# Sign bits of two heads in one matmul run, from two-head tiles loaded for them, with the instruction order drawn anew

## The chip, the cores and the metric

The kernel runs on one core of one Trainium2 chip. The metric is device time in microseconds (us) of one execution, lower is better, as the median of three runs. The engines are named as in the profile: PE is the matrix engine (TensorE), PEld its weight loads, DVE the vector engine, ACT the scalar engine, POOL the GpSimd engine, SP the engine that issues most DMAs.

## The reference

Attention of 2 x 8 heads with 768 tokens of 64 numbers, in which a query sees only the keys of its hash bucket. Then two feed-forward layers on the 1536 x 512 result, the first with a leaky ReLU, the second with a rational function of its input.

```python
def _attn_ref(q, k, v, proj):            # 2 x 8 x 768 x 64, proj 64 x 6
    q_bits = (np.einsum('bhsd,dk->bhsk', q, proj) > 0).astype(np.int64)
    k_bits = (np.einsum('bhsd,dk->bhsk', k, proj) > 0).astype(np.int64)
    powers = 2 ** np.arange(n_bits)      # 6 bits
    mask = np.sum(q_bits * powers, -1)[:, :, :, None] == np.sum(k_bits * powers, -1)[:, :, None, :]
    scores = np.where(mask, scale * np.matmul(q, k.transpose(0, 1, 3, 2)), -1000000000.0)
    attn = np.exp(scores - np.max(scores, axis=-1, keepdims=True))
    attn = attn / (np.sum(attn, axis=-1, keepdims=True) + 1e-09)
    return np.matmul(attn, v)
# layer 1: h = x @ w_in (512 -> 2048); g = max(h,0) + alpha*min(h,0); g @ w_out
# layer 2: h = x @ w_in; P = cubic(h); Q = 1 + |b0||h| + |b1|h*h; (P / (Q + 1e-6)) @ w_out
```

## The kernel before, in words

**Attention.** The 16 heads go one after the other. `head(h)` loads the head's transposed keys and queries, `rk` and `rq` (128 x 768: the head's 64 rows, twice one below the other), makes a rounded copy of each (`k2`, printed as `k`, and `qh`) and the remainders (`kx`, `ql`). The bucket test rides in the score matmul: rows 64 to 75 of `ql` and `k2` hold the 6 sign bits and their complements of each query and key, scaled so that each bit that differs adds a huge penalty.

**Bits.** `bits_mm` (L452) projects the head on the 6 vectors and their negatives in four small matmuls into one PSUM tile `pb`, two column halves of q and two of k; the trace counts each matmul twice. `bits_ev` (L457) turns `pb` into bits `bt` in one DVE instruction, and `move` (L468) copies `bt` by four small DMAs from SP to rows 64 to 75 of `ql` and `k2`; for head 0 DVE writes them there itself (L461). The weights `zq` and `zk` have rows for the upper 64 partitions only, the rest is zero.

**Rows of a head.** For each of 6 tiles of 128 queries: scores `s` on PE (L520, L522), clamp and row maximum `x` on DVE (L528), exponential on ACT (L534), transposition `t` on PE (L552), copy to `pt` (ACT mostly). Then P times V into `pv` (L612, two pieces of 12 trace rows or one of 24), and the row sums: their reciprocals are split in two parts `rr`, turned by PE into `rb` (L584), copied to `rt`, spread by PE (L591), copied to `rs`, and multiplied in (L619, `acc`).

**Layers.** Each weight arrives as 64-bit pieces `raw` that ACT and DVE turn into two 32-bit parts (L304 to L334); in attention about one piece per head is done between the heads' work. Layer 1 and 2 run in units of 512 tokens and a quarter of the hidden width: matmuls `h` (L641), the nonlinearity on ACT, DVE and POOL (L677 to L721), its two parts `gh` and `gl`, matmuls `o` (L657 in layer 1, L660 in layer 2), and a sum on DVE (L764). Four PSUM buffers `h` hold the hidden values until `gl` (L419) has been made.

**Order.** Nothing of the order is written by hand. `plan.add` hands over tasks with the buffers that they read and write and a duration for each engine that may do them; `Plan.order` is a list scheduler that gives every task an engine and a place. The table `FAVOUR` shifts each kind of task: a number added to its rank, and a factor on its duration by engine. Another table gives another order, and other engines for the copies. A DMA is queued on SP in the planned order, and SP waits at each for its buffer. `CAP` sets the number of buffers, and `SP` here is also the name of a DRAM scratch (`sp`).

Of the kernel before, what the change touches and what calls it, by code (L numbers as in the profile page):

```python
# [14 lines left out]
ALU = mybir.AluOpType  # L15
# [17 lines left out]
PAD = 16  # L33
# [9 lines left out]
CAP = {"raw_qk": 2, "qh": 2, "kx": 2, "ql": 2, "k2": 2, "bt": 2, "vr": 2,  # L43
# [26 lines left out]
    "backb": (12.5, {"act": 0.05, "dvp": 0.48}), "banks": (-9.8, {"none": 1.11}), "bits": (6.4, {"pe": 2.45}),  # L70
    "bits0": (307.2, {"pe": 1.69}), "bits_at": (284.5, {"dvp": 0.31}), "bits_ev": (25.3, {"dvp": 0.3}),
    "bits_evb": (30.6, {"dvp": 2.87}), "bits_mv": (-7.6, {"dma": 2.11}), "bits_mvb": (47.1, {"dma": 0.57}),
    "bitsb": (451.7, {"pe": 0.94}), "c_abs": (293.3, {"act": 0.63}), "c_bits": (-40.2, {"dve": 5.95}),
    "c_hi": (-2525.5, {"act": 0.33, "dve": 0.06, "pool": 0.4}), "c_lo": (-27.6, {"dve": 0.24}),
    "c_load": (191, {"dma": 0.12, "none": 3.41}), "c_prep": (673.4, {"dve": 0.7}), "c_tail": (1.1, {"act": 0.38}),
    "clamp": (24.3, {"dvp": 2.08}), "clampb": (-181.2, {"dvp": 8.19}), "e_abs": (65.7, {"act": 2.31}),
    "e_bits": (-1115.9, {"dve": 0.36}), "e_lo": (15.6, {"dve": 1.15}), "e_load": (124.3, {"dma": 0.27}),
    "e_out": (415.1, {}), "e_tail": (-137.8, {"act": 0.42}), "expo": (30, {"act": 0.67}), "expob": (0, {"act": 1.51}),
    "eye": (-1276, {"dma": 2.17}), "eye_prep": (333.9, {"act": 0.02, "dve": 0.04, "pool": 0.04}),
# [5 lines left out]
    "g_lo0": (0, {"dvp": 0.28}), "g_lo1": (-1009.1, {"dvp": 1.07}), "g_lo2": (130.7, {"dvp": 0.85}),
    "g_neg": (-317, {"act": 1.54}), "g_neg0": (-112.5, {"act": 6.17}), "g_neg1": (-1.8, {"act": 7.94}),
    "guard": (86.4, {}), "guardb": (-505.3, {"dve": 1.6}), "k2": (0, {"act": 3.0, "dve": 0.42, "pool": 0.18}),
    "k20": (97, {"act": 0.02, "dve": 50.0, "pool": 0.19}), "k2b": (145.6, {"act": 0.74, "dve": 5.4, "pool": 1.68}),
    "kx": (0.7, {"dve": 2.0}), "kx0": (-2.6, {}), "kxb": (-355, {"dve": 8.17}), "load": (-1817.5, {"dma": 8.2}),
    "load0": (0, {"dma": 0.78, "none": 0.34}), "loadb": (66.1, {"dma": 2.11}), "o_add1": (-656.2, {"dvp": 2.93}),  # L90
    "o_add2": (-19.4, {}), "o_ev": (-181.6, {"act": 1.85, "dvp": 1.35}), "o_ev0": (150.6, {"act": 0.07, "dvp": 50.0}),
    "o_ev2": (330.1, {"act": 0.22, "dvp": 1.37}), "over": (-33.2, {"dvp": 0.04}), "overb": (-457.4, {"dvp": 0.48}),
    "part1": (-74.5, {"act": 4.65, "dve": 0.09, "pool": 0.81}),
    "part1b": (13.8, {"act": 4.7, "dve": 0.03, "pool": 2.52}), "part2": (52.2, {"dve": 9.8, "pool": 4.83}),
# [160 lines left out]
def lsh_attention_moe_moe(ctx: ExitStack, tc: tile.TileContext, qT, kT, vN, consts, eye,  # L255
# [119 lines left out]
    cp.tile([128, PAD], F32, name="pad")  # L375
# [11 lines left out]
    Z = [hp.tile([128, 32], F32, name=f"z{n}") for n in "qk"]  # L387
# [35 lines left out]

    def head(h):
# [33 lines left out]

        def bits_at(n):
            to, j, r = T["ql" if n < 2 else "k2"], n % 2, slice(32 * n, 32 * n + 2 * NB)  # L460
            v_.tensor_scalar(to[64:64 + 2 * NB, j * HALF:(j + 1) * HALF], T["b"][r, :HALF],  # L461
                             cst[r, 0:1], cst[r, 1:2], op0=ALU.is_ge, op1=ALU.mult)

        def move(n):
            def f(e):
                for j in range(2):
                    r = 64 * n + 32 * j
                    nc.sync.dma_start(out=T[("ql", "k2")[n]][64:64 + 2 * NB, j * HALF:(j + 1) * HALF].bitcast(F32),  # L468
                                      in_=T["bt"][r:r + 2 * NB].bitcast(F32))
            return f  # L470
# [531 lines left out]
```

## Time and profile before

| | |
|---|---|
| median of 3 runs | 775.31 us (774.53 to 777.95) |
| the profiled execution | 774.81 us, of which its span 773.0 us |
| PE busy | 760.3 us, 98% of the span |
| DVE, ACT, POOL busy | 650.1 (84%), 542.5 (70%), 147.7 (19%) |
| granted PE clock | 0.998 of full speed |
| attention | until about 256 us; layer 1 until about 495 us, layer 2 after it |

The time is 1.81 us more than the span, which runs from the first to the last instruction. An engine's busy time counts overlapping instructions once.

### The profile page before, as it was taken

How to read it: one execution, taken by the hardware profiler on the slowest of the kernel's cores; microseconds unless marked ns; L12 is line 12 of the kernel's file. 1: busy time of each engine (PE TensorE's matmuls, PEld its weight loads, DVE VectorE, ACT ScalarE, POOL GpSimd, SP SyncE). 2: the span in 40 equal slices, each digit the busy share in tenths (PEclk: the TensorE clock that was granted, in tenths of full speed). 3: DMA queues.
4: the chain of work that ended last, by engine and by line, in shares of the span. 5: the costliest groups of instructions: out<-in, count | busy, mean ns of one | idle time of the engine just before them, and what ended most of it. 6: DMA issues, size and time to landing. Idle time of an engine off the chain costs nothing.

```text
span 773.0 us, 11054 instructions
## 1 busy us (share of the span) xinstructions
PE 760.3 (98%) x3868; PEld 600.4 (78%) x3868; DVE 650.1 (84%) x1208; ACT 542.5 (70%) x945; POOL 147.7 (19%) x135
## 2 busy tenths in 40 slices
PE   8999999999999999999999999989999999999998
PEld 6776777677677788888888888868888888888886
DVE  6899988988887797998899989998787787787882
ACT  4998898798787465643454455788998887777770
POOL 2231211231300000000000000044333343323330
PEclk9999999999999999999999999999999999999999
DMA  6333434545411223345632563520201400200012
GB/s 211 110 108 124 142 94 146 167 128 168 149 60 42 69 81 109 110 138 162 190 101 91 171 208 97 207 98 39 109 1 52 166 1 1 109 1 2 14 55 95
DMA packets 27127, 79.69 MB, mean 103 GB/s; under 512 B 3696, under 2 KB 4416, under 8 KB 25536
## 3 DMA queue, kind: packets, MB, share of 16 engines
q1 hardware_dynamic: 26784, 78.58, 31.2%
q8 instruction: 30, 0.49, 0.2%
q10 hardware_dynamic: 288, 0.41, 0.2%
q14 instruction: 25, 0.20, 0.1%
HBM read 62.14 MB, written 15.73 MB: 101 GB/s over the span
## 4 chain that ended last, share of the span: by engine, by line
PE 90%; DVE 6%; ACT 2%; issue 1%; DMA 0%; POOL 0%; SPq 0%; DVEq 0%; POOLq 0%
PE h L641 33%; PE o L660 17%; PE o L657 14%; PE pv L612 7%; PE t L552 7%; PE s L520 4%; PE s L522 4%; PE pb L452 2%; PE h L657 1%; DVE x L528 1%; PE warm L790 1%; DVE kx L444 1%; PE rb L591 1%; DVE h L703 1%; DVE acc L619 0%
## 5 line engine op out<-in xcount | busy, mean ns | idle before, releaser
L641 PE MATMUL h<-xh,wih 128*128 128x512 f32 x384 | 150.6, 392 | 2.9 <-DVE gl L419 2.9
L641 PE MATMUL h<-xh,wil 128*128 128x512 f32 x384 | 150.1, 391 | 0.0
L641 PE MATMUL h<-xl,wih 128*128 128x512 f32 x384 | 150.0, 391 | 0.0
L706 POOL TENSOR_TENSOR x<-x,ap 128x512 f32<-128x512 f32 x48 | 62.1, 1295 | 284.9 <-DVE ap L706 283.1
L528 DVE TENSOR_SCALAR_CACHE_REDUCE x<-s 128x768 f32<-128x768 f32 x96 | 91.2, 952 | 7.7 <-PE s L522 6.1
L534 ACT ACTIVATE x<-x,st 128x768 f32<-128x768 f32 x96 | 89.4, 933 | 7.7 <-DVE x L528 7.1
L410 ACT ACTIVATE gh<-h 128x512 fp32r<-128x512 f32 x95 | 56.6, 597 | 47.7 <-DVE h L721 27.8
L641 PEld LDWEIGHTS h<-xh,wih 128*128 128x128 f32 x384 | 72.4, 188 | 18.3 <-DVE gl L419 3.3
L641 PEld LDWEIGHTS h<-xl,wih 128*128 128x128 f32 x384 | 72.5, 189 | 15.2
L641 PEld LDWEIGHTS h<-xh,wil 128*128 128x128 f32 x384 | 72.5, 189 | 15.0
L410 ACT ACTIVATE pt<-t 128x768 f32<-128x768 f32 x96 | 76.6, 804 | 10.6 <-PE t L552 9.8
L552 PE MATMUL t<-eyes,x 128*128 128x128 f32 x576 | 79.9, 276 | 1.2 <-DVE x L528 0.7
L552 PEld LDWEIGHTS t<-eyes,x 128*128 128x128 f32 x576 | 64.5, 141 | 19.3 <-ACT x L534 9.9
L660 PE MATMUL o<-woh,gh 128*128 128x512 f32 x192 | 74.7, 389 | 0.0
L660 PE MATMUL o<-woh,gl 128*128 128x512 f32 x192 | 74.7, 389 | 0.0
L660 PE MATMUL o<-wol,gh 128*128 128x512 f32 x192 | 74.7, 389 | 0.0
L419 DVE TENSOR_TENSOR gl<-h,gh 128x512 fp32r<-128x512 f32 x96 | 64.6, 684 | 11.0 <-ACT gh L410 9.9
L657 PE MATMUL o<-gh,woh 128*128 128x512 f32 x176 | 68.5, 389 | 0.0
L657 PE MATMUL o<-gh,wol 128*128 128x512 f32 x176 | 68.5, 389 | 0.0
L657 PE MATMUL o<-gl,woh 128*128 128x512 f32 x176 | 68.5, 389 | 0.0
L612 PE MATMUL pv<-pt,vr 128*64 128x384 f32 x384 | 68.3, 494 | 0.0
L764 DVE TENSOR_TENSOR acc<-acc,o 128x512 f32<-128x512 f32 x72 | 48.9, 681 | 16.9 <-PE o L660 14.7
(114 smaller groups left out, 1488.7 us busy)
## 6 DMA issues: line engine op xcount, KB each, us to landing
raw<-w_in SPq DMA_DIRECT2D x32, 512.0 KB
raw<-w_out SPq DMA_DIRECT2D x32, 512.0 KB
rk<-kT SPq DMA_DIRECT2D x16, 384.0 KB
sp<-mag SPq DMA_DIRECT2D x24, 256.0 KB
rq<-qT SPq DMA_DIRECT2D x15, 384.0 KB
sp<-w SPq DMA_DIRECT2D x16, 256.0 KB
vr<-vN SPq DMA_DIRECT2D x8, 384.0 KB
wih<-sp SPq DMA_DIRECT2D x3, 1024.0 KB
```

The lines of the kernel that those rows point to most:

```text
L410: s_.activation(out, in_, AF.Copy, scale=scale)
L419: eng[e].tensor_tensor(out, a, b, op=ALU.subtract)
L520: te.matmul(sp[:, j, :HALF], K["qh"][:, q], K["kx"][:, j * HALF:(j + 1) * HALF], start=True, stop=False)
L528: v_.tensor_scalar(x.rearrange("p (j c) -> p j c", j=2), T["s"][:, :, :HALF], SCALE, FAR, op0=ALU.mult, op1=ALU.min, accum_out=T["st"])
L534: s_.activation(T["x"], T["x"], AF.Exp, bias=T["st"], scale=-1.0, accum_out=tr["ss"][:, tt, half:half + 1])
L552: te.transpose(o[:, c], T["x"][:, c], idf)
L612: te.matmul(T["pv"][64 * half:64 * half + 64, :HALF], tv["vr"][:, m, kt, :], E[half][0]["pt"][:, kt, :], start=(kt == 0), stop=(kt == NT - 1))
L641: te.matmul(hp, wt[:, kc, f], xt[:, kc], start=(n == 0), stop=(n == 3 * KC - 1))
L657: te.matmul(op, lt[:, m, d], rt, start=(n == 0), stop=(n == 3 * FT - 1))
L660: te.matmul(op, lt[:, d], rt[:, m], start=(n == 0), stop=(n == 3 * FT - 1))
L706: eng[e].tensor_tensor(P[a], P[a], P[b], op=op)
L764: v_.tensor_tensor(a, a, o, op=ALU.subtract if moe else ALU.add)
```

## The change

From head 2 on the bits of two heads (2 and 3, 4 and 5, ...) come from one run. For it the two heads' 64 rows stand one below the other in tiles of their own (`rp`), which two more loads per pair bring from new inputs `kN` and `qN`. The weights get a second block of 12 columns for the lower 64 rows, so `bits_mm` and `bits_ev` stay as they are, 4 matmuls and one evacuation, but yield 24 rows per group instead of 12. The heads' own tiles `rq`, `rk` are still loaded. `bt` has one buffer instead of two and serves both heads' moves; heads 0 and 1 keep their own runs. The `FAVOUR` table is new throughout. The planner's price of a move goes from 1.0 to 1.45.

```diff
-CAP = {"raw_qk": 2, "qh": 2, "kx": 2, "ql": 2, "k2": 2, "bt": 2, "vr": 2,
+CAP = {"raw_qk": 2, "qh": 2, "kx": 2, "ql": 2, "k2": 2, "rp": 2, "bt": 1, "vr": 2,
...
-    "scaled": (312, {"act": 0.17, "dvp": 21.96}), "scaledb": (-242.3, {"act": 2.09, "dvp": 0.42}),
...
+    "s22": (57.1, {}), "scaled": (-33, {"act": 12.9, "dvp": 0.39}), "scaledb": (118.7, {"act": 29.24, "dvp": 0.02}),
...
+        def load2(n, src):
+            def f(e):
+                P[n] = tl(hp, "rp", [128, S], F32, f"{n}{h}")
+                nc.sync.dma_start(out=P[n], in_=src[h // 2])
+            return f
...
-                r = T["rq" if n < 2 else "rk"]
-                te.matmul(T["b"][32 * n:32 * n + 32, :HALF], Z[n // 2], r[:, n % 2 * HALF:(n % 2 + 1) * HALF],
+                r = P["rq" if n < 2 else "rk"]
+                te.matmul(P["b"][32 * n:32 * n + 32, :HALF], Z[n // 2], r[:, n % 2 * HALF:(n % 2 + 1) * HALF],
...
-                    r = 64 * n + 32 * j
+                    r = 64 * n + 32 * j + h % 2 * 2 * NB * (h > 1)
...
-        b = plan.buf("b")
-        plan.add("bits" + z, bits_mm, {"pe": 0.98}, [*R, BZ], [b], cols=1536)
+        if h < 2:
+            P = T
+        elif h % 2 == 0:
+            P = PAIR[h // 2] = {}
+            R = [plan.buf("rp") for n in "kq"]
+            for n, src, r in (("rk", kN, R[0]), ("rq", qN, R[1])):
+                plan.add("load2" + z, load2(n, src), {"dma": 1.1}, writes=[r])
+        else:
+            P = PAIR[h // 2]
+        if h < 2 or h % 2 == 0:
+            b = plan.buf("b")
+            plan.add("bits" + z, bits_mm, {"pe": 0.98}, [*R, BZ], [b], cols=1536)
         if h:
-            bt = plan.buf("bt")
-            plan.add("bits_ev" + z, bits_ev, {"dvp": 0.6}, [b], [bt])
+            if h == 1 or h % 2 == 0:
+                P["B"] = plan.buf("bt")
+                plan.add("bits_ev" + z, bits_ev, {"dvp": 0.6}, [b], [P["B"]])
+            bt = P["B"]
             for n in range(2):
-                plan.add("bits_mv" + z, move(n), {"dma": 1.0}, [bt, *([B["kx"]] * n)], [B[("ql", "k2")[n]]])
+                plan.add("bits_mv" + z, move(n), {"dma": 1.45}, [bt, *([B["kx"]] * n)], [B[("ql", "k2")[n]]])
...
         for z, sign in zip(Z, (1.0, -1.0)):
-            for i in range(2):
-                v_.tensor_scalar(z[0:64, i * NB:(i + 1) * NB], every[0:64, 0:NB], sign * (1 - 2 * i), None, op0=ALU.mult)
+            for m in range(2):
+                for i in range(2):
+                    r, c = slice(64 * m, 64 * m + 64), (2 * m + i) * NB
+                    v_.tensor_scalar(z[r, c:c + NB], every[r, 0:NB], sign * (1 - 2 * i), None, op0=ALU.mult)
...
+        "qN": lay(inputs["q"].reshape(NH, S, D).transpose(0, 2, 1)).reshape(NH // 2, 2 * D, S),
+        "kN": lay(inputs["k"].reshape(NH, S, D).transpose(0, 2, 1)).reshape(NH // 2, 2 * D, S),
```

Line numbers of the changed kernel are 4 higher at `head`'s loads and 22 higher from the rows of a head on.

**PE, in the rows of head 2.** `s_2` and `s_3` are score tiles, `t_0` a transposition, `pb` the bits. Before, the run for head 3 stands here:

```order
L520 MATMUL s_2_545<-kx_323,qh_373 128x384 x2
L522 MATMUL s_2_545<-k_318,ql_109 128x384 x2
L552 MATMUL t_0_556<-eyes,x_0_519 128x128 x6
L452 MATMUL pb_568<-rq_481,zq 32x384 x2
L452 MATMUL pb_568<-rk_448,zk 32x384 x2
L520 MATMUL s_3_576<-kx_323,qh_373 128x384 x2
L522 MATMUL s_3_576<-k_318,ql_109 128x384 x2
```

Now:

```order
L542 MATMUL s_2_562<-kx_326,qh_379 128x384 x2
L544 MATMUL s_2_562<-k_323,ql_108 128x384 x2
L574 MATMUL t_0_571<-eyes,x_0_534 128x128 x6
L542 MATMUL s_3_582<-kx_326,qh_379 128x384 x2
L544 MATMUL s_3_582<-k_323,ql_108 128x384 x2
```

The two `pb` rows are gone. In the whole program `pb` has 36 matmuls instead of 64 (9 runs instead of 16), and `pv` stands in 30 pieces instead of 29.

**SP, the first loads.** Before, with `rk_193`, `rq_208` the tiles of head 1 and `eyes` the identity for the transpositions:

```order
L440 DMA rk_155<-kT 128x768
L502 DMA vr_157<-vN 128x768
L298 DMA raw<-w_in 128x512
L801 DMA eyes<-eye 128x512
L502 DMA vr_175<-vN 128x768
L298 DMA raw<-w_in 128x512
L440 DMA rk_193<-kT 128x768
L440 DMA rq_208<-qT 128x768
```

Now, with `rk_194`, `rq_207` the tiles of head 1 and `rk_175`, `rq_199` those of the pair 2 and 3:

```order
L444 DMA rk_154<-kT 128x768
L301 DMA raw<-w_in 128x512
L524 DMA vr_168<-vN 128x768
L454 DMA rk_175<-kN 128x768
L301 DMA raw<-w_in 128x512
L524 DMA vr_192<-vN 128x768
L444 DMA rk_194<-kT 128x768
L454 DMA rq_199<-qN 128x768
L825 DMA eyes<-eye 128x512
L444 DMA rq_207<-qT 128x768
```

The pair's two tiles stand ahead of head 1's queries, and `eyes` has moved behind head 1's keys.

**DVE, from layer 1 to layer 2.** Before, the last rows up to the second `gl` of layer 2 (`h<-t,bab,h`, `h<-h,qc,aq` and `h<-h,aq` are steps of layer 2's function, `mag`, `raw`, `wol` of a weight piece):

```order
L325 SCALAR_TENSOR_TENSOR mag<-raw 128x512
L703 SCALAR_TENSOR_TENSOR h<-h,aq 128x512
L319 TENSOR_SCALAR mag<-mag 128x512
L327 TENSOR_SCALAR raw<-c 128x512
L321 TENSOR_SCALAR mag<-mag 128x512
L697 SCALAR_TENSOR_TENSOR h<-t,bab,h 128x512
L721 TENSOR_TENSOR h<-x,h 128x512 x2
L764 TENSOR_TENSOR acc_62<-acc_62,o 128x512 x2
L334 SCALAR_TENSOR_TENSOR wol_100<-mag,raw 128x512
L419 TENSOR_TENSOR gl<-h,gh 128x512 x2
```

Now:

```order
L421 TENSOR_TENSOR gl<-h,gh 128x512
L326 SCALAR_TENSOR_TENSOR c<-raw,mag 128x512
L725 SCALAR_TENSOR_TENSOR h<-h,qc,aq 128x512
L322 TENSOR_SCALAR mag<-mag 128x512
L725 SCALAR_TENSOR_TENSOR h<-h,aq 128x512
L324 TENSOR_SCALAR mag<-mag 128x512
L743 TENSOR_TENSOR h<-x,h 128x512
L725 SCALAR_TENSOR_TENSOR h<-h,qc,aq 128x512
L719 SCALAR_TENSOR_TENSOR h<-t,bab,h 128x512
L421 TENSOR_TENSOR gl<-h,gh 128x512
```

From layer 2's first product `ap<-ap,t` to its second `gl` DVE has 34 instructions before and 29 now; PE's matmul groups stand in the same order here. Over the whole program the new table also gives DVE 16 copies `rs<-rb` instead of 5, 8 `ql<-qh,rq` instead of 1, 1 `rr<-ss` instead of 11 and none instead of 7 `rr<-ss,rr`, 5 `rt<-rb` instead of 9, no `qh<-rq` instead of 2, 8 `bt` instead of 15, 8 instructions for `zq` and `zk` instead of 4, and in layer 2 28 `x<-x,ap` instead of none and 33 `ap<-ap,t` instead of 24; those left to POOL are 20 instead of 48 and 15 instead of 24.

## Rows read from the trace of the kernel before

**Rows 1.** Stretches: us; busy PE, PEld, DVE, ACT, POOL (instructions); clock, DMA share, GB/s.

```profile
9.00:30.00 21.00, 17.59 (x102) 13.78 (x102) 19.81 (x41) 15.58 (x30) 6.34 (x6) 1.00 0.36 119
30.00:210.00 180.00, 178.35 (x1214) 124.55 (x1213) 163.16 (x359) 155.73 (x283) 40.74 (x41) 1.00 0.44 134
50.00:90.00 40.00, 39.81 (x272) 27.54 (x271) 38.53 (x86) 35.50 (x67) 9.46 (x12) 1.00 0.40 127
256.00:487.00 231.00, 231.00 (x1021) 191.25 (x1020) 207.33 (x378) 116.18 (x200) 1.24 (x2) 1.00 0.41 130
520.00:740.00 220.00, 220.00 (x964) 182.03 (x965) 171.65 (x266) 181.09 (x309) 80.65 (x63) 0.99 0.12 47
```

**Rows 2.** What PE waited for: us in total, times, longest; the largest.

```profile
PE h L641 <- DVE gl L419: 2.9, 1, 2.9
```

**Rows 3.** The chain that ended last, around two bits runs: start, length, what.

```profile
58.51 0.35 PE s L522 x2
58.86 0.78 PE pb L452 x8
59.64 0.80 PE t L552 x6
...
85.56 0.66 PE t L552 x6
86.21 0.78 PE pb L452 x8
87.00 0.55 PE s L520 x2
```

**Rows 4.** Groups by line and shape: count, busy us and mean ns, idle before.

```profile
L457 DVE TENSOR_SCALAR bt<-pb,every 128x384 fp32r<-128x384 f32 x15 | 10.1, 673 | 1.5 <-PE pb L452 1.5
L414 DVE COPY rs<-rb 128x384 f32<-128x384 f32 x5 | 2.7, 545 | 0.0
L419 DVE TENSOR_TENSOR ql<-qh,rq 64x768 fp32r<-64x768 f32 x1 | 1.0, 951 | 1.2 <-ACT qh L410 1.2
L414 DVE CAST rr<-ss 128x6 fp32r<-128x6 f32 x11 | 3.2, 293 | 0.6
L419 DVE TENSOR_TENSOR rr<-ss,rr 128x6 fp32r<-128x6 f32 x7 | 1.1, 160 | 0.1
L414 DVE CAST rt<-rb 12x128 fp32r<-12x128 f32 x9 | 2.5, 275 | 1.6 <-PE rb L584 1.6
L414 DVE CAST qh<-rq 128x768 fp32r<-128x768 f32 x2 | 1.1, 556 | 0.0
L706 DVE TENSOR_TENSOR ap<-ap,t 128x512 f32<-128x512 f32 x24 | 16.6, 692 | 16.7 <-ACT ap L694 16.5
```

**Rows 5.** The time line ahead of the wait in rows 2: start, length, instruction.

```profile
512.41 1.44 POOL L706 TENSOR_TENSOR ap<-ap,t 128x512 f32<-128x512 f32 x1 [2.00 <-ACT ap L694]
...
512.28 0.42 DVE L319 TENSOR_SCALAR mag<-mag 128x512 f32<-128x512 f32 x1
512.62 1.51 DVE L327 TENSOR_SCALAR raw<-c 128x512 uint32<-128x512 uint32 x1
514.05 1.51 DVE L321 TENSOR_SCALAR mag<-mag 128x512 uint32<-128x512 uint32 x1
```

**Rows 6.** The time line of the first tiles: landings that ended waits, ACT's first exponential.

```profile
10.54 0.65 ACT L308 ACTIVATE raw<-raw 128x512 uint32<-128x512 uint32 x1 [0.97 <-DMA raw<-w_in]
...
12.06 1.06 POOL L412 TENSOR_SCALAR k<-rk 128x768 fp32r<-128x768 f32 x1 [9.23 <-DMA rk<-kT]
...
15.15 0.94 ACT L534 ACTIVATE x<-x,st 128x768 f32<-128x768 f32 x1 [3.96 <-DVE x L528]
```

**Rows 7.** The time line of SP's moves for one head, and its first scores.

```profile
99.75 0.33 SPq L440 DMA_DIRECT2D rk<-kT  x1
...
102.74 1.47 SPq L468 DMA_DIRECT2D k<-bt  x2
...
106.35 0.59 PE L520 MATMUL s<-kx,qh 128*128 128x384 f32 x2
```

More of the change, by code (lines that the diff above doesn't have):

```diff
@@ L70 @@
[L70 to L79, printed above, removed]
@@ L85 @@
[L85 to L94, printed above, removed]
@@ new lines @@
+    "a_n2": (95.9, {"dvp": 0.84}), "a_p0": (-107.9, {"act": 3.65}), "a_p1": (-1736.7, {"act": 4.27}),
+    "a_prep": (-194.9, {}), "a_quad": (255.2, {"dvp": 0.98}), "a_sq": (-261.1, {"act": 2.63}),
+    "a_sum": (2279.3, {"dve": 0.07, "pool": 0.09}), "back": (274.2, {"act": 0.11, "dvp": 0.1}),
+    "backb": (58, {"act": 0.06, "dvp": 12.89}), "banks": (0, {"none": 1.11}), "bits": (346.6, {"pe": 2.45}),
+    "bits0": (211.4, {"pe": 1.69}), "bits_at": (-91.8, {"dvp": 0.31}), "bits_ev": (-316.4, {"dvp": 0.3}),
@@ new lines @@
+    "bits_evb": (0, {"dvp": 2.87}), "bits_mv": (12.7, {"dma": 2.11}), "bits_mvb": (-273.9, {"dma": 0.57}),
+    "bitsb": (91.1, {"pe": 0.94}), "c_abs": (-4.9, {"act": 0.63}), "c_bits": (95.1, {"dve": 5.95}),
+    "c_hi": (-503.4, {"act": 0.14, "dve": 0.03, "pool": 0.75}), "c_lo": (224.1, {"dve": 0.24}),
+    "c_load": (0, {"dma": 0.12, "none": 3.41}), "c_prep": (-9.9, {"dve": 0.7}), "c_tail": (-3.2, {"act": 0.38}),
+    "clamp": (-114.9, {"dvp": 2.08}), "clampb": (31.5, {"dvp": 8.19}), "e_abs": (505.1, {"act": 2.31}),
@@ new lines @@
+    "k20": (-173.3, {"act": 27.15, "dve": 6.82, "pool": 0.81}),
+    "k2b": (499.9, {"act": 0.02, "dve": 3.04, "pool": 0.03}), "kx": (-11.8, {"dve": 2.0}), "kx0": (-47.6, {}),
+    "kxb": (630.3, {"dve": 8.17}), "load": (12.6, {"dma": 8.2}), "load0": (63.4, {"dma": 0.78, "none": 0.34}),
+    "load2": (-185.6, {}), "load2b": (739.3, {}), "loadb": (-9.7, {"dma": 2.11}), "o_add1": (-1156.9, {"dvp": 2.93}),
+    "o_add2": (-17.3, {}), "o_ev": (205.6, {"act": 0.02, "dvp": 0.35}),
+    "o_ev0": (-518.2, {"act": 0.02, "dvp": 14.13}), "o_ev2": (125.4, {"act": 0.02, "dvp": 16.79}),
@@ new lines @@
+    "over": (-27.7, {"dvp": 0.04}), "overb": (-6.3, {"dvp": 0.48}),
+    "part1": (372.8, {"act": 0.03, "dve": 1.44, "pool": 3.09}),
+    "part1b": (-119.9, {"act": 0.04, "dve": 0.04, "pool": 16.03}), "part2": (-19.1, {"dve": 20.21, "pool": 0.14}),
+    "part2b": (-223.5, {"dve": 40.41, "pool": 0.02}), "pv": (-1426.8, {"pe": 1.11}), "pvb": (-1793.9, {}),
+    "qh": (-1018.2, {"act": 0.7, "dve": 2.98, "pool": 1.89}),
+    "qh0": (-12.9, {"act": 1.28, "dve": 6.94, "pool": 1.38}), "qhb": (-108, {"act": 2.22, "dve": 0.19, "pool": 0.06}),
@@ new lines @@
+    "scores": (-756.2, {"pe": 2.11}), "scoresb": (-431.8, {}), "spread": (7.8, {"pe": 2.26}),
+    "spreadb": (213.4, {"pe": 0.46}), "store": (-47.7, {}), "swap": (205.5, {}),
+    "take": (57, {"act": 0.17, "dvp": 4.39}), "takeb": (0, {"act": 3.25, "dvp": 26.81}),
+    "turn": (748.7, {"pe": 0.19}), "turnb": (-179.2, {"pe": 3.96}), "u_abs": (1021.6, {"act": 3.87}),
+    "u_bits": (-6.1, {}), "u_hi": (-15.7, {"act": 0.07, "dve": 6.47, "pool": 0.82}), "u_lo": (1.7, {"dve": 0.17}),
+    "u_load": (-346.3, {"dma": 0.33}), "u_tail": (297.4, {"act": 1.39}), "v_load": (-31.4, {"dma": 0.51}),
@@ L254, in lsh_attention_moe_moe @@
 @with_exitstack
-def lsh_attention_moe_moe(ctx: ExitStack, tc: tile.TileContext, qT, kT, vN, consts, eye,
+def lsh_attention_moe_moe(ctx: ExitStack, tc: tile.TileContext, qT, kT, qN, kN, vN, consts, eye,
                           w_in1, w_out1, w_in2, w_out2, out):
@@ L374, in lsh_attention_moe_moe @@
     rt = cp.tile([128, 128], F32R, name="rt")
-    cp.tile([128, PAD], F32, name="pad")
+    Z = [cp.tile([128, 32], F32, name=f"z{n}") for n in "qk"]
     att = ExitStack()
@@ L921, in swap_rest @@
         more(o=ps2, h2=ps2, mag2=mp, w322=cp, ap=mp, aq=mp)
-    for f, b, tags in ((swap, BS[1], ("raw_qk", "qh", "kx", "ql", "k2", "bt")),
+    for f, b, tags in ((swap, BS[1], ("raw_qk", "qh", "kx", "ql", "k2", "rp", "bt")),
                        (swap_rest, BS[2], ("x", "pt", "vr", "st", "ss", "rr", "rt", "rs", "s", "b", "pv", "h"))):
@@ L970 @@
     for n in range(4):
-        cst[32 * n + n // 2 * NB:32 * n + (n // 2 + 1) * NB, 0] = TINY
+        for m in range(2):
+            c = 32 * n + (2 * m + n // 2) * NB
+            cst[c:c + NB, 0] = TINY
         cst[32 * n:32 * n + 32, 1] = PEN if n > 1 else 1.0
```

69 lines of the change are left out of this document (32 added, 37 removed).

## The prediction

> **What bounds the kernel now.** I read the stretches first [rows 1]. PE is busy all the time from 256 to 487 us and from 520 to 740 us, and 178.35 of 180 us in attention proper (30 to 210 us). DVE comes next, with 163.16 of these 180 us, 90.6%. So a microsecond of PE work that goes from attention comes off the end, as long as DVE doesn't take over; where PE stands idle, a better order can give something back. The idle times lie at the start (3.4 us between 9 and 30 us), in attention (1.65 us), between the layers and at the very end. Of PE's named waits only one is long [rows 2]: 2.9 us for `gl` on DVE, once, where layer 2 begins. The sum is made against the profiled execution, 774.81 us (a span of 773.0 us and 1.81 us around it).
>
> **The removed bits runs.** Seven of 16 runs go, those of heads 3, 5, ... 15. In the chain a run takes 0.78 us from its start to the next group [rows 3]. The group behind it pays too: six transpositions take 0.80 us there and 0.66 us elsewhere, two score matmuls 0.55 us and 0.35 us elsewhere. That is 0.14 to 0.20 us more, so 0.95 us a run, 6.65 us for seven. One more piece of `pv` costs one such extra, 0.20 us. Left: **-6.45 us**, if PE's work sets the end there; nothing, if DVE does. These runs are matmul work that nothing covers, so no cover is lost with them.
>
> **DVE in attention.** By the counts of the two orders and the means of the groups [rows 4] DVE loses 7 `bt` (4.71 us), 10 `rr` (2.93), 7 `rr` remainders (1.12), 4 `rt` (1.10) and 2 `qh` (1.11), and gains 11 `rs` (6.00), 7 `ql` (6.66) and 4 small ones for the weights (at most 0.6, priced as `rr` remainders): about +2.3 us, though seven evacuations went. About 1.9 of it fall in the 180 us of the stretch, which then holds 165.1 us of DVE work. PE's part of that stretch falls by six runs, to 174.3 us: 94.7% for DVE. From 50 to 90 us DVE is at 38.53 of 40 us, 96.3%, and PE idles 0.19 us there [rows 1]. So PE can stay the bound at such a load. DVE alone, at 96.3%, would need 171.4 us, which is less than PE's 174.3. Tighter it gets all the same: between `rb` and its spread PE now has a single group (0.66 or 0.70 us [rows 3]) for 14 of 16 heads by the order, for 8 before, and most `rt` copies are ACT's. I take **+1.0 us** of new waits. Bounds: nothing, as in the 50 to 90 us stretch, and 3.4 us, what PE idles from 9 to 30 us, where DVE is at 94.3% and the pipeline has no reserve [rows 1].
>
> **The start.** Fourteen loads of 384 KB come on, two of them into the busiest time. In the trace the second `raw` lands at 10.54 us and head 1's keys, next in the queue, at 12.06 us [rows 6]: 384 KB in 1.52 us, an estimate of 253 GB/s. Ahead of those keys the queue now holds 2560 KB instead of 2432 KB (+0.5 us), and behind them the pair's queries and `eyes`, 640 KB, come before head 1's queries (+2.5 us). By this estimate `eyes` lands at about 15.1 us and head 1's queries at about 16.6 us (13.6 before). ACT works in order and has the two copies of `eyes` and head 1's `qh` ahead of its first exponential, which would start after 16.6 us instead of at 15.15 us. Behind ACT wait the transpositions on PE, and PE itself stands at head 1's bits, now ahead of `s_2`. That is 1.5 us or more; the 3.4 us that PE idles up to 30 us take some of it. I take **+1.0 us**, from 0 to 3.0, the whole delay of head 1's queries. The 12 later loads are 4.6 MB more in 200 us, beside 134 GB/s at a DMA share of 0.44 [rows 1]; they find their place, and I cost them at nothing. Their cover is the whole head of time that a pair's tile has before its run.
>
> **Between the layers.** The 2.9 us wait [rows 2] is for the second `gl` of layer 2, which frees the PSUM buffer of the next `h`. Up to it DVE has 34 instructions after layer 2's first product, now 29. At 0.42 to 0.69 us each [rows 4, 5] the five are 2.1 to 3.5 us less, and PE's groups keep their order. Besides, two DVE instructions took 1.51 us each while POOL multiplied, where one of the same shape a moment before took 0.42 us [rows 5]: 2.2 us lost. The new order gives several of these products to DVE at this place. Either alone is worth about the wait. On the other side DVE itself now does the products, and ACT's steps lie between. I take **-2.5 us**, from -2.9 (the wait gone) to 0 (it comes back at another buffer). In layer 2 the 37 products that move from POOL to DVE cost 25.6 us of DVE (0.692 each): 197.3 of 220 us, 89.7%. From 256 to 487 us DVE is at 207.33 of 231, as much, and PE has no idle time [rows 1], so I cost them at nothing.
>
> The Trainium skill, Advanced Engine Details and Errata, VectorE Performance Modes, says that GpSimd shares the vector engine's second SBUF port and that two-port vector instructions and GpSimd's block each other. By that rule taking products off POOL frees DVE, and this term would be the full wait, for a sum 0.4 us lower; the 1.51 us rows agree with it.
>
> **The moves** of the bits are as many as before (60 small DMAs). An odd head's wait only for its own `kx`, a head of time ahead. An even head's stand behind the load of the next pair's keys, as they stood behind the next head's keys (99.75 us), with the last pair of moves issued by 104.21 us and the head's first scores at 106.35 us [rows 7], and PE waited for none of them. Between a pair's run and those scores PE has, by the order, both pieces of a `pv` and at least five score or transposition groups now, no less than before. Nothing.
>
> **Sum.** 774.81 - 6.45 + 1.0 + 1.0 - 2.5 = 767.9 us for an execution like the profiled one. The median of the runs is 0.5 us above that execution, so **768.4 us**, 0.9% less.
>
> **The rivals.** *DVE and ACT become the bound in attention.* For it speaks the 94.7%, and that DVE's work grows while PE's falls; against it the 50 to 90 us stretch. With 3.4 us of new waits, the wait between the layers kept and the start as forecast: 774.81 - 6.45 + 3.4 + 1.0 + 0.5 = 773.3 us (775.3 with the start at its bound), no change that can be told. 0.5%, 3.9 us, is about what a measurement of this kernel can tell. The same time comes out if removed runs turn into idle time: the change then does its work and gains nothing. Chance 0.17.
>
> *Even heads' bits arrive late* (the other side). The load ahead of the moves is new, `bt` has one buffer, and SP works in order. If each of the seven even heads had one more 384 KB load to wait for (1.52 us [rows 6]), PE would stand at the first scores for up to 10.6 us: 774.81 - 6.45 + 10.6 + 1.0 - 2.5 + 1.0 + 0.5 = 779.0 us. It decides from about 1 us a head (no gain left) and makes the kernel measurably slower from 1.5 us on. Against it: one such load stood there before, PE never waited, and PE's work in between has not shrunk. Chance 0.07.
>
> *A clean gain*: the new table also closes the gaps at the start and in attention. 774.81 - 6.45 - 2.9 + 0.5 = 766.0 us, and up to 1.7 us less if half of the 3.4 us go too. Chance 0.16. The forecast itself, 766 to 771.4 us, has 0.60.
>
> **Range and chances.** The bounds of the terms give 764.5 us (a clean gain with nearly half of the start's idle time) to 774.0 us (the first rival, between its two times); it leaves out the second rival and some of the first. Faster by over 0.5% (under 771.4 us): 0.76. Within 0.5%: 0.17. Slower: 0.07.
>
> **What would show it.** PE's busy time about 6 us lower, all of it in attention; `pb` with 72 trace rows instead of 128. No wait of PE for `gl` where layer 2 begins, or one under 1 us. The first exponential on ACT some 2 us later. In attention PE's idle time below 3 us, with DVE at about 95%. I would be wrong if PE's waits for `x`, `rt` or `pt` in attention summed to over 4 us, if `k` or `ql` moves ended waits of PE at first scores, or if a new wait of some us stood in layer 2, where DVE now does the products.

## The result and the profile after

| | before | changed |
|---|---|---|
| median | 774.98 us (774.53 to 777.95, 4 runs) | 767.34 us (765.54 to 768.25, 4 runs) |
| ratio | | 0.989, 95% interval 0.9859 to 0.9922 |
| span of the profiled execution | 773.0 us | 763.8 us |
| PE, DVE, ACT, POOL busy | 760.3, 650.1, 542.5, 147.7 | 754.0, 673.9, 537.8, 91.1 |
| start of the last head's `pv` | 251.52 us | 244.73 us |
| from there to the end | 521.5 us | 519.1 us |

The changed kernel is 7.6 us faster by the medians, 9.2 us by the two profiled executions; that of the changed kernel, at 765.54 us, is the fastest of its four. The forecast was 768.4 us. The last two rows of the table divide the span: the last `pv` piece of 24 trace rows ends attention, and 2269 trace rows of PE lie from it to the end in both kernels. In these two executions 6.8 us came from ahead of that mark, 2.4 us from behind it.

The stretches of the changed kernel (columns as in [rows 1]; the layers are shifted by the time gained):

```profile
9.00:30.00 21.00, 17.52 (x106) 12.85 (x106) 19.35 (x40) 16.15 (x31) 7.05 (x7) 1.00 0.53 173
30.00:210.00 180.00, 178.58 (x1202) 128.72 (x1202) 169.47 (x363) 158.96 (x298) 24.31 (x31) 1.00 0.51 156
50.00:90.00 40.00, 39.89 (x272) 28.28 (x271) 37.08 (x83) 35.97 (x67) 6.23 (x7) 1.00 0.44 142
249.00:480.00 231.00, 231.00 (x1014) 190.13 (x1014) 205.99 (x375) 117.27 (x203) 2.94 (x3) 1.00 0.41 128
513.00:731.00 218.00, 218.00 (x961) 179.97 (x960) 190.71 (x297) 180.70 (x308) 41.49 (x33) 1.00 0.13 50
```

In attention DVE is busy for 94.2% of the time (90.6% before), and PE stands idle for 1.42 us of 180 (1.65 before). In layer 2 DVE works 190.7 of 218 us and PE has no idle time. The clock, 0.99 in the last row of [rows 1], is 1.00.

What PE waited for in the changed kernel, all waits of 0.4 us and more (us in total, times, longest):

```profile
PE s L544 <- DVE k L471: 2.3, 1, 2.3
PE warm L812 <- POOL zq L837: 1.0, 1, 1.0
PE t L574 <- DVE x L550: 0.8, 2, 0.5
PE s L542 <- ACT pt L412: 0.8, 1, 0.8
PE pb L462 <- DMA rq<-qT: 0.4, 1, 0.4
PE rb L606 <- POOL rr L421: 0.4, 1, 0.4
```

No wait for `gl` [rows 2] is left. The 2.3 us lie at the first scores of all, which wait for head 0's bits, written in place by DVE.

PE's and DVE's groups that answer to the change and to [rows 4] (columns as there):

```profile
L462 PE MATMUL pb<-rq,zq 128*32 128x384 f32 x36 | 8.9, 575 | 0.4 <-DMA rq<-qT 0.4
L462 PE MATMUL pb<-rk,zk 128*32 128x384 f32 x36 | 8.9, 575 | 0.0
```

```profile
L728 DVE TENSOR_TENSOR ap<-ap,t 128x512 f32<-128x512 f32 x33 | 23.0, 697 | 15.5 <-ACT ap L716 15.3
L728 DVE TENSOR_TENSOR x<-x,ap 128x512 f32<-128x512 f32 x28 | 19.3, 690 | 1.0 <-POOL ap L728 0.4
L416 DVE COPY rs<-rb 128x384 f32<-128x384 f32 x16 | 8.8, 552 | 0.2
L421 DVE TENSOR_TENSOR ql<-qh,rq 64x768 fp32r<-64x768 f32 x8 | 7.5, 940 | 0.0
L467 DVE TENSOR_SCALAR bt<-pb,every 128x384 fp32r<-128x384 f32 x8 | 5.4, 674 | 0.0
```

`pb` has 72 trace rows instead of 128, and the added products in layer 2 cost DVE what the mean of before said, 0.69 us each.

The time line of the changed kernel at its start, which answers to [rows 6], and its last `pv` piece:

```profile
9.89 0.66 ACT L311 ACTIVATE raw<-raw 128x512 uint32<-128x512 uint32 x1 [2.55 <-DMA raw<-w_in]
...
12.11 0.83 POOL L414 TENSOR_SCALAR k<-rk 128x768 fp32r<-128x768 f32 x1 [2.77 <-DMA rk<-kT]
...
13.80 0.31 ACT L412 ACTIVATE ident<-eyes 128x128 fp32r<-128x128 f32 x1 [3.25 <-DMA eyes<-eye]
...
14.78 0.84 ACT L412 ACTIVATE qh<-rq 128x768 fp32r<-128x768 f32 x1 [0.25 <-DMA rq<-qT]
...
14.89 0.86 PE L462 MATMUL pb<-rq,zq 128*32 128x384 f32 x2 [0.42 <-DMA rq<-qT]
...
15.63 0.94 ACT L556 ACTIVATE x<-x,st 128x768 f32<-128x768 f32 x1
...
16.33 0.62 PE L542 MATMUL s<-kx,qh 128*128 128x384 f32 x2
...
37.37 0.62 PE L542 MATMUL s<-kx,qh 128*128 128x384 f32 x2
...
244.73 4.09 PE L634 MATMUL pv<-pt,vr 128*64 128x384 f32 x24
```

Head 1's keys are used at 12.11 us, as early as before (12.06), although the second `raw` no longer stands right ahead of them. The first exponential starts 0.5 us later than before, not 2. The row at 37.37 us is the first score group of head 2, which stands at 37.45 us in the kernel before. This execution is one with a quick start; the repeat below has another.

### The profile page after: what moved, and what is told of

Its sections match the earlier page's. It is cut to its first block, busy times and chain, and to the rows that moved or that the text cites. A ratio compares the mean times of both kernels' runs of the same rounds, so it can differ in the third digit from the quotient of the medians.

```text
span 763.8 us, 10842 instructions
## 1 busy us (share of the span) xinstructions
PE 754.0 (99%) x3812; PEld 597.7 (78%) x3812; DVE 673.9 (88%) x1239; ACT 537.8 (70%) x949; POOL 91.1 (12%) x97
## 4 chain that ended last, share of the span: by engine, by line
PE 87%; issue 2%; DVE 1%; ACT 1%; POOL 0%; POOLq 0%
PE h L663 34%; PE o L682 17%; PE o L679 16%; PE t L574 6%; PE pv L634 6%; PE s L542 3%; PE s L544 3%; PE h L679 1%; PE pb L462 0%; PE rb L613 0%; DVE x L550 0%; ACT x L556 0%; DVE kx L448 0%; DVE acc L641 0%; ACT pt L412 0%
## 5 line engine op out<-in xcount | busy, mean ns | idle before, releaser
L550 DVE TENSOR_SCALAR_CACHE_REDUCE x<-s 128x768 f32<-128x768 f32 x96 | 91.1, 951 | 7.3 <-PE s L544 6.5
L412 ACT ACTIVATE gh<-h 128x512 fp32r<-128x512 f32 x92 | 53.9, 599 | 38.8 <-DVE h L743 23.0
L311 ACT ACTIVATE raw<-raw 128x512 uint32<-128x512 uint32 x64 | 43.1, 673 | 30.4 <-DMA raw<-w_in 18.1
```

The source lines that it names most:

```text
L311: s_.activation(self.low, self.low, AF.Copy, scale=2.0 ** -9 * (1 - 2.0 ** -22))
L412: s_.activation(out, in_, AF.Copy, scale=scale)
L550: v_.tensor_scalar(x.rearrange("p (j c) -> p j c", j=2), T["s"][:, :, :HALF], SCALE, FAR, op0=ALU.mult, op1=ALU.min, accum_out=T["st"])
```

## The experiments

Every kernel was timed in five rounds beside the kernel before, whose medians there were 775.3 to 775.8 us. "Mark" is the start of the last `pv` piece of 24 rows. Executions of one kernel differ at the start: in some PE's score groups still take 0.84 us at 20 us. The profiled execution of the changed kernel is one with the early start; its repeat (the second experiment) is one with the late start, and is what the marks and busy times of late ones are held against. Where medians are compared, "the changed kernel" is the 767.5 us of that repeat.

### The parts alone

**The paired bits under the table of before**, everything else as changed (one line of the table stands for all):

```diff
-    "s22": (57.1, {}), "scaled": (-33, {"act": 12.9, "dvp": 0.39}), "scaledb": (118.7, {"act": 29.24, "dvp": 0.02}),
+    "scaled": (312, {"act": 0.17, "dvp": 21.96}), "scaledb": (-242.3, {"act": 2.09, "dvp": 0.42}),
...
```

> The changed kernel with the table of numbers of the kernel before: the pairing alone. Theory (seven runs of matmul work go from a path that PE sets): PE busy about 6.4 us lower than before, the 2.9 us wait between the layers still there or moved, 766 to 771 us. Rival (the new table is what gives the time): the pairs without their own table leave new waits in attention that eat most of it, 773 us or more.

Measured: 799.34 us, ratio 1.0322 (1.03 to 1.0344): 24.1 us slower than before, far outside the theory's range. PE's largest waits:

```profile
PE rb L602 <- DVE rr L417: 5.6, 2, 3.1
PE s L538 <- ACT pt L408: 4.4, 6, 1.4
PE rb L602 <- POOL rr L417: 4.4, 3, 2.5
PE h L659 <- DVE gl L417: 2.9, 1, 2.9
```

The first three stand in attention, behind copies, in the order that the old table gives for the new program; the last is the wait of [rows 2]. Two of its stretches:

```profile
28.00:32.00 4.00, 4.00 (x21) 4.00 (x20) 3.90 (x9) 3.67 (x8) 0.93 (x2) 0.58 0.51 180
...
30.00:210.00 180.00, 166.79 (x1092) 118.43 (x1090) 157.75 (x325) 148.11 (x271) 45.42 (x45) 0.99 0.50 155
```

PE idles 13.2 us of 180, and in some stretches the granted clock is down as well. The mark stands at 278.60 us.

**The changed kernel again**, unchanged:

> The changed kernel once more, beside the others of this call: 766 to 768.5 us by every theory. Its trace tells how much the landing of head 1's queries at the start differs from one execution to the next.

Measured: 767.52 us (765.66 to 768.01), ratio 0.9895 (0.9878 to 0.9912). Its profiled execution has a span of 766.0 us, a mark at 247.00 us and 519.0 us behind it: the 2.2 us above the first profile lie ahead of the mark. Its time line at the start:

```profile
15.12 0.85 PE L462 MATMUL pb<-rq,zq 128*32 128x384 f32 x2 [0.66 <-DMA rq<-qT]
...
16.56 1.01 PE L542 MATMUL s<-kx,qh 128*128 128x384 f32 x2
17.36 0.84 PE L544 MATMUL s<-k,ql 128*128 128x384 f32 x2
...
19.93 0.84 PE L544 MATMUL s<-k,ql 128*128 128x384 f32 x2
...
21.42 0.59 PE L542 MATMUL s<-kx,qh 128*128 128x384 f32 x2
...
39.66 0.61 PE L542 MATMUL s<-kx,qh 128*128 128x384 f32 x2
```

PE waits 0.66 us for head 1's queries here (0.42 in the first profile), and the first score groups take 1.01 and 0.84 us up to 21 us; in the first profile the group at 16.33 us takes 0.62. Head 2's first scores (39.66 us) are 2.3 us later than there; from them to the mark it is 207.34 us here and 207.36 there.

**The new table with the bits runs of before:**

```diff
-    "scaled": (312, {"act": 0.17, "dvp": 21.96}), "scaledb": (-242.3, {"act": 2.09, "dvp": 0.42}),
+    "s22": (57.1, {}), "scaled": (-33, {"act": 12.9, "dvp": 0.39}), "scaledb": (118.7, {"act": 29.24, "dvp": 0.02}),
...
```

> The kernel before, with 16 bits runs, under the new table of numbers: the table alone. Theory: no run is saved, so PE's busy time stays at about 760 us; at best the 2.9 us wait between the layers goes: 772 to 777 us. Rival (the table gives the time): 770 us or less.

Measured: 782.06 us, 1.0091 (1.0075 to 1.0107). Its mark is at 263.99 us, 12.5 us later than before, but behind it are only 516.7 us instead of 521.5: the wait for `gl` is gone. So the table's part in the layers works without the pairs, and its part in attention doesn't. Neither half of the change, taken as it stands, is worth anything in attention without the other.

### Work added and taken away in place

In these five the order of all other instructions is that of the kernel they start from.

**Each pair's bits run done twice** (changed kernel):

```diff
             for n in range(4):
...
+            for n in range(4 * (h > 1)):
+                r = P["rq" if n < 2 else "rk"]
+                te.matmul(P["b"][32 * n:32 * n + 32, :HALF], Z[n // 2], ...)
```

> The changed kernel with each of the 7 pair runs done twice in place, same order of all else, same result. Theory (PE sets the end in attention, DVE at 94% or not): 7 x 0.64 to 0.78 us longer, 771.5 to 773 us, all of it as PE busy time. Rival (DVE or ACT set the end there by now): under 1.5 us longer, the rest falls into PE's idle time.

Measured: 771.59 us, 0.9951 (0.9932 to 0.997), 4.1 us above the changed kernel; mark 251.36 us, 4.4 us behind that of the repeat. The `pb` rows take 13.50 us of PE instead of 8.98, 0.65 more a run; PE's whole busy time is 759.4 us, 3.3 above the repeat's 756.1. Of the 4.4 us 1.3 lie ahead of head 2's first scores (40.92 us), with a longer wait for head 1's queries:

```profile
16.36 0.85 PE L462 MATMUL pb<-rq,zq 128*32 128x384 f32 x2 [1.89 <-DMA rq<-qT]
```

From there to the mark it is 210.44 us, 3.1 more than in the repeat, with 3.3 us more of PE's time. So added PE work comes through in full there, and the median lies in the theory's range.

**The same for heads 3, 5, ... 15 in the kernel before** (`range(4 * (h > 2 and h % 2))` and `T` instead):

> The kernel before in its own order, with the bits runs of heads 3, 5, ... 15 done twice in place (8 matmuls instead of 4, the same result). Theory (a run costs its PE time in the old order too, when added): 5.4 to 6.7 us more than the kernel before, 780.5 to 782 us. Rival (in the old order PE has slack at these places because another engine is later, as the small gain from leaving the runs out suggested): under 3 us more, 776 to 778.5 us.

Measured: 778.53 us, 1.0039 (1.0024 to 1.0053), 2.8 us above before. Its profile has the mark 5.5 us later than before, of which the start accounts for about 1.3 (its third score group is at 22.02 us instead of 20.67). So about 4 us by the mark, between the two theories, as in the changed kernel; the median alone, 2.8 us, would fall to the rival.

**The bits runs of heads 3, 5, ... 15 left out of the kernel before:**

```diff
+            if h > 2 and h % 2:
+                used["b"] += 1
+                T["b"] = eyes.rearrange("p a b -> p (a b)")
+                return
             T["b"] = tl(ps, "b", [128, 512], F32, f"pb{h}")
```

> The kernel before, same order, without the matmuls of the bits runs of heads 3, 5, ... 15; their evacuation reads a constant tile instead, so these heads get bits that are not theirs, and all else is done as before. Theory (each run and the switch behind it is 0.95 us on the path): 6 to 6.7 us faster than before, 768.5 to 769.5 us. Rival (DVE, ACT or the planned places of all else hold the pace, and PE's time turns into waits): under 3 us faster.

Measured: 773.15 us, 0.9982 (0.9964 to 1.0), 2.4 us below before by the medians and 1.1 us by the mark (250.42). The theory that a removed run counts in full fell here. The stretch, and waits of PE:

```profile
30.00:210.00 180.00, 175.98 (x1172) 124.18 (x1172) 162.75 (x361) 155.90 (x285) 41.88 (x41) 1.00 0.44 135
```

```profile
PE h L645 <- DVE gl L419: 2.9, 1, 2.9
PE s L524 <- ACT pt L410: 2.6, 5, 0.8
...
PE t L556 <- DVE x L532: 1.2, 4, 0.5
```

PE's work became idle time: 4.0 us of 180 instead of 1.65, in short waits for `pt` and `x`. And the evacuation from the constant tile takes DVE 0.47 us instead of 0.67, 1.4 us less for seven, so even the 1.1 us need not be PE's. Behind the mark this execution takes 522.8 us, 1.3 more than before, so as a whole (775.02 us) it is no faster than the profiled one before.

**The runs of all seven pairs left out of the changed kernel** (the same edit with `h > 1` and `P`):

> The changed kernel in its own order, with the four matmuls of all seven pairs' bits runs left out; the evacuation reads the constant eyes tile in their place, so the bucket bits of heads 2 to 15 are not computed, while loads, moves and everything else stay. Theory (PE sets the pace in the changed order, so bits runs count in full there): 7 x 0.78 to 0.95 us less, 761 to 762.5 us. Rival (behind PE another chain, DVE or ACT, lies so close that removed runs turn into idle time, as when the odd heads' runs were left out of the kernel before): 764.5 to 766 us, with PE's idle time in attention 3 us or more above the 1.42 us of 30 to 210 us.

Measured: 766.49 us (764.49 to 766.92), 0.988 (0.9857 to 0.9904), 1.0 us below the changed kernel; mark 245.93 us, 1.1 before that of the repeat, though PE's busy time falls by 5.2 us (756.1 to 750.9). The time lies 0.5 us above the rival's range; its mechanism is there:

```profile
30.00:210.00 180.00, 175.05 (x1156) 128.18 (x1155) 168.86 (x364) 159.99 (x299) 24.24 (x32) 1.00 0.49 156
```

PE idles 4.95 us instead of 1.42; its waits for `x` (DVE) sum to 3.0 us instead of 0.8, those for `pt` (ACT) to 1.8 instead of 0.7. Here too DVE's evacuations are shorter, by 1.4 us.

**The evacuations of the pairs three times, and not at all** (changed kernel):

```diff
+            for _ in range(1 + 2 * (h > 1)):
-            v_.tensor_scalar(P["bt"], P["b"][:, :HALF], ...)
+                v_.tensor_scalar(P["bt"], P["b"][:, :HALF], ...)
```

```diff
+            if h > 1:
+                used["bt"] += 1
+                P["bt"] = eyes.rearrange("p a b -> p (a b)")[:, :HALF]
+                return
             P["bt"] = tl(hp, "bt", [128, HALF], F32R, f"bt{h}")
```

> The changed kernel in its own order, with each of the six or seven pairs' evacuations bt done three times by DVE (0.67 us each, 8 to 9.4 us more DVE work in attention, the same result). Theory (PE is the bound and DVE at 94% has room for short bursts): under 3 us more, 767.5 to 770.5 us. Rival of the prediction (DVE at 94 to 95% is as good as the bound): the added DVE work comes through nearly in full, 6 to 9 us more, 773.5 to 777 us, with PE's waits for DVE (x, rt, k) grown by as much.

> The changed kernel in its own order, with all bits runs kept on PE but the seven pairs' evacuations bt left out of DVE (7 x 0.67 = 4.7 us); the moves copy rows of the constant eyes tile in their place, so the bucket bits of heads 2 to 15 are not used. Theory (after the run with the evacuations done three times, which cost over 1 us per us of added DVE work: DVE sets the pace of attention in this order, at 94%, while PE's runs taken out gave about 1 us): 4 to 6 us less, 761.5 to 763.5 us. Rival (PE at 99% sets the pace, and DVE counts only when it is loaded further): under 1.5 us less, 766 to 767.5 us. A gain in between says that both are bound in turn.

Measured: three times, 778.02 us, 1.0031 (1.0017 to 1.0045): 10.5 us above the changed kernel for 14 x 0.67 = 9.4 us of DVE work, more than the rival's 6 to 9 (mark 258.14, 11.1 us behind the repeat's). Not at all, 766.49 us (764.83 to 768.04), 0.9885 (0.9856 to 0.9914): 1.0 us less for 4.7 us. In the first the stretch and PE's largest waits are:

```profile
30.00:210.00 180.00, 171.21 (x1148) 122.28 (x1148) 169.40 (x358) 153.98 (x284) 23.59 (x30) 1.00 0.48 150
```

```profile
PE rb L607 <- POOL rr L421: 5.6, 4, 1.8
PE t L575 <- DVE x L551: 4.4, 7, 1.1
```

DVE does no more in 180 us than in the changed kernel (169.4 and 169.5 us); PE idles 8.8 us. In the second, DVE's time falls:

```profile
30.00:210.00 180.00, 179.03 (x1210) 129.37 (x1202) 166.39 (x357) 159.32 (x299) 23.97 (x32) 1.00 0.51 156
```

and PE is busy for 179.03 of 180 us. So in this order both are bound. Either of them relieved alone gives about 1 us, which the intervals of the ratios don't tell from nothing; either one loaded further costs 0.9 us (PE, 4.1 for 7 x 0.65) or 1.1 us (DVE) per us of work.

### The layers and the start

**The changed kernel with the entries of before for the two products of layer 2** (the two entries alone, out of longer lines)**:**

```diff
-"a_mul": (-395.2, {"dve": 0.39, "pool": 0.48})
+"a_mul": (-301, {"dve": 0.07, "pool": 0.07})
-"a_sum": (2279.3, {"dve": 0.07, "pool": 0.09})
+"a_sum": (-23.4, {"dve": 0.77, "pool": 0.02})
```

> The changed kernel with the two table entries for layer 2's products (the multiplication and the sum) of the kernel before; all instructions ahead of layer 2 stand as in the changed kernel. Theory (the wait between the layers went because DVE has less to do there and POOL no longer slows it): a wait of PE for gl of 2 to 3 us comes back, 769 to 770.5 us. Rival (the wait went because the order of attention and layer 1 is another): within 0.5 us of the changed kernel, no wait.

Measured: 770.61 us, 0.9943 (0.9927 to 0.9959), 3.1 us above the changed kernel; 522.3 us behind the mark instead of 519.1. The wait is back, at two `h` buffers:

```profile
PE h L663 <- DVE gl L421: 2.7, 2, 1.7
```

**The opposite: the kernel before with the new entries.**

> The kernel before with the two table entries for layer 2's products of the changed kernel; all instructions ahead of layer 2 stand as before. Theory (these two entries alone take the wait between the layers away): no wait of PE for gl, 2 to 3 us faster than before, 772 to 773.5 us. Rival (the wait went with the order ahead of it): within 0.7 us of before.

Measured: 779.64 us, 1.006 (1.0041 to 1.008), 4.1 us slower than before. The wait grew, and the granted clock fell in it and behind it:

```profile
PE h L641 <- DVE gl L419: 6.3, 1, 6.3
```

```profile
524.00:528.00 4.00, 0.00 (x0) 0.00 (x0) 4.00 (x8) 3.90 (x8) 3.30 (x3) 0.53 0.00 0
528.00:532.00 4.00, 3.89 (x11) 3.14 (x12) 4.00 (x8) 0.94 (x2) 0.00 (x0) 0.62 0.00 0
```

So the products on DVE are needed for the gain between the layers, but only with the places that the new table gives to the rest.

**The first pair's two loads put behind head 1's queries** (changed kernel; `LATE` keeps the two loads until `rq` of head 1 has been issued):

```diff
+                if (n, h) == ("rq", 1):
+                    for g in LATE:
+                        g()
...
+                LATE.append(g) if h == 2 else g()
```

> The changed kernel with the first pair's two loads issued behind head 1's queries; all other instructions in the same order. Theory (the two loads in the busiest time cost about 1 us at the start): eyes and head 1's queries land 1 to 2 us earlier, PE no longer waits for the queries, 0.5 to 1.5 us faster. Rival (the start is set by DVE and ACT work, not by landings): within 0.5 us of the changed kernel.

Measured: 766.45 us (765.62 to 766.81), 0.9886 (0.9869 to 0.9902). The median is 0.9 to 1.1 us below those of the changed kernel, but the intervals of the ratios overlap nearly whole and the profiled spans are equal (763.8 us). It is the best version run that computes everything, by less than can be told. In its profile `eyes` lands at 12.52 us instead of 13.80 and head 1's queries at 14.58 instead of 14.78; PE waits 0.23 us for them, and the start is an early one (head 2's first scores at 37.41 us).

## Why the prediction was right

**The removed bits runs: size right, reason incomplete.** PE's busy time fell by 6.3 us (forecast 6.45): ahead of the mark from 245.4 to 238.9 us (760.3 - 514.87 and 754.0 - 515.14). Between head 2's first scores and the mark the time fell by 6.7 us (214.07 to 207.36) and PE's busy time in it by 6.5, in the repeat as well. But the step "a microsecond of PE work that goes from attention comes off the end, as long as DVE doesn't take over" is wrong for a fixed order: seven runs (5.5 us) taken out in place give about 1 us in either kernel. PE at 99% looked like the bound; it is one of two engines that wait for one another in turn, each in a written-out order. The change removes a run on PE and an evacuation on DVE together, and the table puts everything else at other places. That pairs and table need one another is shown by the two halves (24.1 and 6.8 us slower); that the removed evacuations relieve DVE is not, for its work between those two points rose, from 189.67 to 194.47 us. Which places in the new order turn the removed runs into time stays open. How much a run and its evacuation, taken out of one place together, would give without a new table was not tried, nor what a table drawn anew for the kernel before would give alone.

**DVE in attention: +1.0 forecast, nothing came.** Its share was forecast well (94.7%, measured 94.2%), though its work ahead of the mark rose by 4.1 us (218.9 to 223.0) and not by 2.3; but PE's idle time went from 1.65 to 1.42 us. The rival "DVE and ACT become the bound" was nearer than its chance of 0.17 says: DVE at 94% is as good as bound, as the tripled evacuations show. The new order has no reserve there, but PE's waits did not grow in it.

**The start: +1.0 forecast; nothing came in the first profile, about 2 us in the repeat.** The path is the one forecast: PE stands at head 1's bits for head 1's queries, 0.42 us in the first profile, 0.66 in the repeat and 1.89 with the doubled runs. Of the seven profiled executions with the loads of the change the first profile alone, with the shortest wait, had the early start. The other six waited 0.58 us or more, and their head 2 began at 39.1 to 41.7 us (two of them with added work ahead of it); four in the order of before began it at 36.95 to 38.85. So +1.0, from 0 to 3.0, is a fair size. That a wait of some tenths goes with 2 us at head 2 is what the rows show; why the score groups then stay at 0.84 us until 20 or 21 us is open.

The step that failed is the 253 GB/s, taken from the landing of `raw` at 10.54 and of the keys at 12.06 us [rows 6]. In the changed kernel the pair's queries and `eyes`, 640 KB, land within 1.69 us behind the keys (12.11 to 13.80), an estimate of 379 GB/s. Nor were the keys held up by the transfers ahead of them alone. SP issues them as late as this, before and in the changed kernel:

```profile
8.71 0.33 SPq L440 DMA_DIRECT2D rk<-kT  x1
...
8.72 0.33 SPq L444 DMA_DIRECT2D rk<-kT  x1
```

That is over 5 us after the load before them (3.10 and 3.09 us), and between 10 and 11 us the queues of the kernel before moved 240 GB/s, in the next microsecond 415. The keys land between 12.06 and 13.92 us in the four executions in the order of before and between 12.11 and 13.76 us in the seven of the change, so the 128 KB more ahead of them are not seen.

**Between the layers: -2.5 forecast, -2.4 measured** (521.5 to 519.1 us behind the mark), out of three terms of which the prediction had one, so the agreement is in part luck. The wait is gone (2.9 us by [rows 2]). The prediction missed that the granted clock of the kernel before falls behind this wait:

```profile
520.00:524.00 4.00, 4.00 (x13) 3.16 (x14) 4.00 (x7) 2.40 (x5) 2.54 (x2) 0.67 0.89 377
524.00:528.00 4.00, 4.00 (x18) 3.25 (x17) 2.67 (x6) 3.56 (x7) 0.18 (x1) 0.90 0.00 0
528.00:532.00 4.00, 4.00 (x19) 3.34 (x18) 3.47 (x6) 4.00 (x9) 2.59 (x2) 1.00 0.00 0
```

At 0.67 and 0.90 of full speed these 8 us lose 4 x 0.33 + 4 x 0.10 = 1.7 us, an estimate from the two rows, which hold 13 and 18 matmuls where the third has 19; it stood in [rows 1] as 0.99. Both together, 4.6 us, are about what the new table gives without the pairs (521.5 to 516.7). In the changed kernel 2.1 us go again: PE's busy time behind the mark is 515.14 us, with the same table and the old runs 512.99. With that table and the old runs the groups of twelve `h` matmuls in layer 1 take 2.72 us each in the chain, in the changed kernel 2.76, in the same grouping. Why is open. The reason given for the term (products moved to DVE, fewer instructions ahead of `gl`) held in the new order: with the old entries 2.7 us of waits return.

The Trainium skill, Advanced Engine Details and Errata, VectorE Performance Modes (the second SBUF port that DVE and GpSimd share), made this term the full wait; the wait is indeed gone. The experiment that put the products back on POOL brought it back, but moved work and places with them, so no run here shows the port by itself.

**What cost nothing, as forecast:** the products on DVE (PE has no idle time in 218 us of layer 2), the 12 later loads (DMA share 0.51 in attention) and the moves. PE never waited for a move, so the rival "even heads' bits arrive late" didn't occur; under the old table `k` moves did end 0.9 us of waits. The other side came by a way that no rival named: with an order that is not drawn for it, the same change is 24 us slower.

For the first profile the sum is 774.81 - 6.8 - 2.4 = 765.6 us (765.54): the +2.0 us for DVE and the start did not come. For the repeat, which is near the median, it is 774.81 - 6.7 + 2.2 - 2.5 = 767.8 us (767.84), with the start at 37.45 and 39.66 us. There the +1.0 us for DVE is missing and the start cost 1.2 us more than forecast. That the median came within 1.1 us of 768.4 is in part luck: these two errors set one another off, and the -6.45 came out right for a reason that is incomplete.

## What to carry to other kernels

A busy share of 99% does not make an engine the only bound: before pricing removed work in full, ask which engine is second, and whether the removed piece relieves both at the same place; adding work in place shows which engines are bound, taking it away in place shows what relief is worth in that order, and neither prices a new order. A change of structure and the order found for it are one change; each half alone can be slower. A wait of PE of some us can cost more than its length, so read the granted clock of the stretch behind it. One profile can show a start that most executions don't have: take a second one before a term is called absent.

## What the runs showed that was not expected

- Taking 5.5 us of PE work or 4.7 us of DVE work out of the same order gave 1.0 us each, while adding 4.5 and 9.4 us cost 4.1 and 10.5 us.
- Behind waits of PE of 2.9 and 6.3 us the granted clock was 0.67 and 0.62 in the stretches of 4 us in which PE worked again; 2.4 GHz is its full level, 1.2 GHz the lower one. Three more kernels with a wait of 2.9 us for `gl` had 0.50 to 0.65 there; the two waits of 1.7 and 1.0 us of the changed kernel with the old entries left it at 1.00.
- The executions of one kernel differ by about 2 us at the start: a score group of two matmuls takes 0.84 us instead of 0.51 until 16 us in one and until 21 us in another, while the clock column reads 1.00. In the changed kernel's order the late ones are those in which PE waited 0.58 us or more for head 1's queries; what follows from the wait is not shown further. With the pair's loads issued later all five runs lay within 1.2 us.
- The pair's queries and `eyes` (384 and 256 KB) landed at about 379 GB/s, 1.5 times the rate that one pair of landings had suggested.
